# Linear attention, top-1 experts and a dense layer on one core: load order, mask selections, list of output rows and expert 0's preparation rearranged

## The chip, the core and the metric

The kernel runs on one core of a Trainium2 chip. The metric is the device time of one launch in microseconds (us); lower is better. The engines are named as in the profile: PE is TensorE's matmul, PEld its weight load, DVE is VectorE, ACT is ScalarE, POOL is GpSimd, and SP is SyncE, which here only issues transfers (its queue is SPq).

## The reference

Three stages follow each other; the output of each is the input of the next. Sizes: 4 batches, 8 heads, 768 positions, 48 features a head; 3072 tokens of 384 features; 8 experts with 1024 hidden units; a last dense layer with 2048.

```python
for t in range(S):                       # 1. gated linear attention
    state = alpha[:, :, t, :, None] * state + einsum('bhd,bhe->bhde', k[:, :, t], v[:, :, t])
    y[:, :, t] = einsum('bhd,bhde->bhe', q[:, :, t], state)
...
expert_idx = argmax(x @ w_gate, axis=1)  # 2. one expert for each token
gate_w = softmax probability of that expert
out[mask] = gate_w[mask, None] * (maximum(xe @ w1[e], 0.0) @ w2[e])
...
h = x @ w_in                             # 3. dense layer
return (h * sigmoid(h)) @ w_out
```

## The kernel before

**Attention (0 to about 130 us of the span).** The 32 heads are handled as 16 pairs, `p` = 0 to 15, four pairs to a batch. The inputs come in 13 tiles `T` (`place`): four for batch 0, three for each other batch, whose fourth pair is packed into spare partitions of the three and copied out by POOL-queue transfers (`gather_last`, L523). The loop over `p` (from L1014) writes the order of the instructions by hand, and every engine runs its own in that order. For a tile, DVE scans the products of the alphas forwards (`P_SCAN`, L538) and backwards (`R_SCAN`, L556) and scales the keys (`K_SCALE`, L561); POOL scales the queries (`Q_SCALE`, L550). For a pair, PE makes the scores of six chunks of 128 positions in two groups of three (`scores`, L583); they are masked to the lower triangle either by one DVE product (L589) or, for group 0 of pairs 1 to 4 and group 1 of pair 14 (`beside_scans`), by an ACT copy (L602) and a POOL `affine_select` (L606) that is issued after the pair's `Q_SCALE`. PE sums the state updates (`updates`, L619 and L626), DVE scans the states (L636), ACT copies them (L653), and PE makes the outputs (`from_states`, `within`).

**Loads.** All loads go through SP's queue in program order. `load(T, "aqk")` brings the alphas, queries and keys of a tile (12 transfers a tile from tile 4 on), at the top of an iteration; `load_v(p + 3)` brings the values of a pair at the end of iteration `p`. Alphas have 3 buffers, values 4.

**Routing.** When a batch's outputs are there, its logits are made (L712), each token gets its expert and a slot, 512 slots to an expert, from a running count `carry` and the offsets `e512` (`ranks` to `slots2`, L784 to L803). The small sum `cb` (L788) adds the two. A table of the token in each slot (`tab`) is made by one-hot matrices on DVE and six matmuls for each batch (`table`, L834 to L872). The tokens' rows are turned, scaled by their gate and stored to DRAM (`rows`, L915 to L920).

**Hand-over (about 130 to 168 us).** Expert 0 works on its first 192 tokens (`F1(t, 0, CA)` and `S1(t, 0, CA)` for six of its eight weight tiles) while batch 3 is still routed; beside that run the ranking of the experts by size (`turns`), the table in that order (`in_turn`), the splits of the weight tiles into a high and a low part (`w_split`: ACT L331, DVE L332), and three gathers of expert 0's other rows (L346). Those rows are turned by PE and split (`x_tile`: PE L356, ACT L358, DVE L359): tile 1 just before the last `S1`, tiles 2 and 3 after it. Then the columns from 192 on follow.

**Experts and dense layer (to the end).** `F1` (L1211: 9 matmuls into `hp`) and `S1` (L1243: 9 matmuls into three banks) alternate for 64 weight tiles `g`; then `F2` and `S2` for 64 steps of the dense layer. The raw weights stream through four buffers (`next_load`, L327 and L1175 on SP's queue). From step 2 on, one step of the list `late` is issued in each `g` that is not the last of its expert: `offsets`, and then for each of the four batches six steps (`packed`) that make `sidx`, the token of each packed output row, by one-hot matrices on DVE and six matmuls into `pt` (L860). `sidx` is first needed by the scatter of the output (L1444).

The lines at the heart of the change are these.

```python
load_v(p + 3)
...
later = [mask_aside(p, 0)] if beside_scans(p, 0) else []
...
3: [last["in_turn"], lambda: w_split(6), lambda: w_split(7)],
...
late = [offsets] + [f for b in range(B) for f in packed(b)]
```

Of the kernel before, what the change touches and what calls it, by code (L numbers as in the profile page):

```python
# [229 lines left out]
def gla_moe_kernel(  # L230
# [23 lines left out]
    x_f = dr.tile([NP, NC, CH, 2 * D], F32, name="x_f")  # L254

# [112 lines left out]
    gidx = const.tile([128, 4 * E], U32, name="gidx")  # L368
    gidx_a = const.tile([128, 2], U32, name="gidx_a")
# [15 lines left out]
    with actx:  # L385
# [70 lines left out]
        load(2, "k")  # L456
        load_v(2)
        Z1 = ac.tile([128, SP], F32, name="Z1")
# [18 lines left out]
        def constants():  # L477
            nc.gpsimd.iota(iota_i, pattern=[[1, 128]], base=0, channel_multiplier=0)
            nc.gpsimd.iota(prow_i, pattern=[[128, NTILE]], base=0, channel_multiplier=1)
            nc.gpsimd.memset(ones, 1.0)  # L480
            nc.gpsimd.memset(onesf, 1.0)
            nc.gpsimd.memset(tri, -1.0)
            nc.gpsimd.affine_select(
                out=tri, in_=tri, pattern=[[-1, 128]], compare_op=ALU.is_ge, fill=0.0, base=0, channel_multiplier=1
            )
            nc.gpsimd.memset(rmask, 1.0)
            nc.gpsimd.memset(ones8, 1.0)
            nc.gpsimd.memset(rmask[:, :, 0:1], 0.0)
            nc.gpsimd.memset(carry, 0.0)
            nc.gpsimd.tensor_copy(iota_f, iota_i)  # L490
            nc.gpsimd.tensor_scalar(w8, iota_f[:, 0:E], -1.0, float(E), op0=ALU.mult, op1=ALU.add)
            nc.gpsimd.tensor_scalar(e512, iota_f[:, 0:E], float(TM), None, op0=ALU.mult)

        def more_constants():
# [4 lines left out]
            nc.gpsimd.tensor_copy(keys, w8)  # L499
# [100 lines left out]
        def mask_aside(p, g, hs=slice(0, 2)):  # L600
            m = st[p]["m", g][:, hs]
            nc.scalar.copy(m, st[p]["Ap"][:, hs])  # L602
            return lambda: select(m)
# [116 lines left out]
        def route(b):  # L720
# [58 lines left out]
            def ranks():  # L779
# [7 lines left out]
                r["cb"] = rt.tile([128, E], F32, tag="cb", name="cb")  # L787
                nc.vector.tensor_tensor(r["cb"], carry, e512, op=ALU.add)  # L788

            def slots1():  # L790
# [4 lines left out]
                    r["cb"].unsqueeze(2).to_broadcast([128, E, TB]),  # L795
# [32 lines left out]
        def table(bk, sl, b, nhi, acc, res, eng):  # L828
# [35 lines left out]
            def add():  # L864
                if b == 0:
                    nc.vector.tensor_copy(acc, r["pt"])
                elif b < B - 1:
                    nc.vector.tensor_tensor(acc, acc, r["pt"], op=ALU.add)
                else:
                    nc.vector.tensor_tensor(acc, acc, r["pt"], op=ALU.add)  # L870
                    n = 4 if acc is tab else NTILE
                    nc.vector.tensor_scalar(res[:, 0:n], acc[:, 0:n], float(NT - 1), None, op0=ALU.min)  # L872
# [25 lines left out]
        def in_turn():  # L898
# [9 lines left out]
            t = rt.tile([128, E * 4], F32, tag="tt", name="tt", bufs=1)  # L908
            nc.vector.tensor_reduce(t, m.rearrange("p r k e -> p (r k) e"), axis=AX.X, op=ALU.add)
            nc.vector.tensor_scalar(gidx[:, 4:], t[:, 4:], float(NT - 1), None, op0=ALU.min)  # L910
# [103 lines left out]
        for p in range(NP + 1):  # L1014
            on, oy = p < NP, p >= 1
            if p in loads:
                load(loads[p])
# [10 lines left out]
            if on:  # L1028
                ks_transpose(p, 0, 3)
                later = [mask_aside(p, 0)] if beside_scans(p, 0) else []  # L1030
# [24 lines left out]
            if on:  # L1055
                for c in range(3, 6):
                    scores(p, c)
                if beside_scans(p, 1):
                    later.append(mask_aside(p, 1))
# [32 lines left out]
            load_v(p + 3)  # L1092
# [10 lines left out]
    with mctx:  # L1103
# [162 lines left out]
        for step in choose:  # L1266
# [6 lines left out]
            3: [last["in_turn"], lambda: w_split(6), lambda: w_split(7)],  # L1273
# [3 lines left out]
        for t in range(part):  # L1277
# [5 lines left out]
            for step in beside.get(t, []):  # L1283
                step()
            if t == part - 1:
                x_tile(0, 1, CA - 128)
# [5 lines left out]
        x_tile(0, 2, bk=4)  # L1292
        x_tile(0, 3, bk=3)
        for t in range(4, NF):
            next_load()
        F1(*seq[0])
# [7 lines left out]
        off = const.tile([128, E], F32, name="off")  # L1304
# [3 lines left out]
        def offsets():  # L1308
            m = rt.tile([128, E, E], F32, tag="m8", name="m8", bufs=1)
            by_turn(carry, m, cnt)  # L1310
# [4 lines left out]
            nc.vector.tensor_tensor(  # L1315
                m, turn.rearrange("p r e -> p e r"), o.unsqueeze(1).to_broadcast([128, E, E]), op=ALU.mult
            )
            nc.vector.tensor_reduce(off, m, axis=AX.X, op=ALU.add)
# [32 lines left out]
        tabc = const.tile([128, NTILE], F32, name="tabc")  # L1351

        def packed(b):
            r = {}

            def slot():
                co = rt.tile([128, E], F32, tag="cb", name="co")
                nc.vector.tensor_tensor(co, off, e512, op=ALU.subtract)
                t1 = rt.tile([128, E, TB], F32, tag="t1", name="t1")
                nc.vector.tensor_tensor(t1, OH[b], co.unsqueeze(2).to_broadcast([128, E, TB]), op=ALU.mult)  # L1360
                r["s"] = sc = rt.tile([128, TB], F32, tag="sc", name="sc")
                nc.vector.tensor_reduce(sc, t1.rearrange("p e i -> p i e"), axis=AX.X, op=ALU.add)
                nc.vector.tensor_tensor(sc, sc, SLOT[b], op=ALU.add)

            digits, hots, invert, add = table(lambda: 3, lambda: r["s"], b, NTILE, tabc, sidx, nc.vector)
            return [slot, digits, hots, lambda: None, invert, add]

        late = [offsets] + [f for b in range(B) for f in packed(b)]
# [85 lines left out]
        for i, (g, c0, c1) in enumerate(seq):  # L1454
            e, f = divmod(g, NF)
            F1(*seq[i + 1]) if i + 1 < len(seq) else F2(0)
            doubles(g, 1)
# [110 lines left out]
```

## Time and profile before

| what | value |
|---|---|
| time, median of 3 runs | 784.77 us (783.9 to 785.85) |
| the profiled execution, whole | 786.41 us |
| its span, first to last instruction | 784.7 us |
| PE busy | 767.6 us, 98% of the span, 5068 matmuls |
| PEld busy | 698.6 us, 89% |
| DVE busy | 476.9 us, 61% |
| ACT busy | 361.8 us, 46% |
| POOL busy | 160.5 us, 20% |
| mean granted TensorE clock | 0.996 |
| chain that ended last | PE 85%, DMA 5%, DVE 4%, issue 3% |

Busy times are sums over the whole span. The chain is followed back from the last instruction, at each step to what released it. A matmul's end is modelled, so a busy PE is not a PE at its peak; what a step costs is read from the starts of successive groups.

### The profile page before, as it was taken

How to read it: one execution, taken by the hardware profiler on the slowest of the kernel's cores; microseconds unless marked ns; L12 is line 12 of the kernel's file. 1: busy time of each engine (PE TensorE's matmuls, PEld its weight loads, DVE VectorE, ACT ScalarE, POOL GpSimd, SP SyncE). 2: the span in 40 equal slices, each digit the busy share in tenths (PEclk: the TensorE clock that was granted, in tenths of full speed). 3: DMA queues.
4: the chain of work that ended last, by engine and by line, in shares of the span. 5: the costliest groups of instructions: out<-in, count | busy, mean ns of one | idle time of the engine just before them, and what ended most of it. 6: DMA issues, size and time to landing. Idle time of an engine off the chain costs nothing.

```text
span 784.7 us, 13301 instructions
## 1 busy us (share of the span) xinstructions
PE 767.6 (98%) x5068; PEld 698.6 (89%) x5068; DVE 476.9 (61%) x818; ACT 361.8 (46%) x684; POOL 160.5 (20%) x201
## 2 busy tenths in 40 slices
PE   8999899999999999999999999999999999999996
PEld 6887788899999999999899899889899898899896
DVE  8989886657797787788687333343443343343332
ACT  1656466435455545555544334453544445233222
POOL 5754322312242232212112200020020001002002
PEclk9999999999999999999999999999999999999999
DMA  9888893624465555655121110031022001001001
GB/s 231 215 200 215 220 262 112 223 61 138 152 185 169 173 172 171 192 168 184 61 60 33 41 39 18 0 94 36 1 76 53 19 1 40 2 1 41 1 0 45
DMA packets 41642, 80.54 MB, mean 103 GB/s; under 512 B 5640, under 2 KB 19863, under 8 KB 41568
## 3 DMA queue, kind: packets, MB, share of 16 engines
q1 hardware_dynamic: 37568, 67.56, 29.8%
q0 software_dynamic: 4000, 12.03, 5.1%
q8 instruction: 42, 0.69, 0.4%
q14 instruction: 32, 0.26, 0.1%
HBM read 68.03 MB, written 9.44 MB: 99 GB/s over the span
## 4 chain that ended last, share of the span: by engine, by line
PE 85%; DMA 5%; DVE 4%; issue 3%; ACT 1%; SPq 1%; POOL 1%; POOLq 0%; ACTq 0%; DVEq 0%
PE hp L1211 38%; PE both L1422 12%; PE ob L1422 12%; PE both L1243 9%; PE yb L1243 5%; PE Ap L583 2%; PE Yp L664 1%; DVE Pf L538 1%; PE xt L356 1%; PE Yp L679 1%; DMA a__371<-in_alpha_dram 1%; PE Xt L915 1%; DMA E<-in_k_dram 1%; DMA a__1156<-in_alpha_dram 1%; PE Lp L712 1%
## 5 line engine op out<-in xcount | busy, mean ns | idle before, releaser
L1211 PE MATMUL hp<-xh,wh 128*128 128x512 f32 (+10 forms) x498 | 184.0, 371 | 0.4 <-ACT xh L358 0.4
L1211 PE MATMUL hp<-xh,wl 128*128 128x512 f32 (+10 forms) x498 | 184.1, 372 | 0.1
L1400 DVE TENSOR_TENSOR sg<-hp,sg 128x512 f32<-128x512 f32 (+1 forms) x97 | 66.5, 686 | 157.3 <-ACT sg L1399 152.5
L1211 PE MATMUL hp<-xl,wh 128*128 128x512 f32 (+10 forms) x498 | 130.8, 371 | 0.0
L1399 ACT ACTIVATE sg<-hp 128x512 f32<-128x512 f32 (+1 forms) x97 | 57.6, 593 | 154.3 <-PE hp L1211 153.5
L1211 PEld LDWEIGHTS hp<-xl,wh 128*128 128x128 f32 x498 | 91.8, 190 | 13.5
L1211 PEld LDWEIGHTS hp<-xh,wh 128*128 128x128 f32 x498 | 94.1, 189 | 10.5 <-ACT xh L358 0.6
L1211 PEld LDWEIGHTS hp<-xh,wl 128*128 128x128 f32 x498 | 94.4, 190 | 9.5 <-DVE wl L332 0.3
L1410 DVE TENSOR_TENSOR hl<-sg,hh 128x512 fp32r<-128x512 f32 x94 | 65.1, 692 | 61.5 <-PE ob L1422 38.4
L1409 ACT CAST hh<-sg 128x512 fp32r<-128x512 f32 x94 | 58.3, 620 | 70.7 <-DVE sg L1400 70.7
L1223 ACT ACTIVATE hh<-hp 128x464 fp32r<-128x464 f32 (+9 forms) x70 | 34.2, 488 | 114.8 <-PE hp L1211 110.6
L1444 POOL DMA_INDIRECT out_dram<-o,sidx x24 | 24.6, 1023 | 278.9 <-ACT o L1442 274.4
L1138 POOL TENSOR_TENSOR wl<-dx,wh 128x384 fp32r<-128x384 f32 x32 | 39.2, 1225 | 197.7 <-ACT wh L1135 194.2
L332 DVE TENSOR_TENSOR wl<-raw,wh 128x768 fp32r<-128x768 f32 x63 | 62.2, 991 | 7.9 <-ACT wh L331 6.9
L1422 PE MATMUL both<-wh,hh 128*128 128x384 f32 x188 | 64.1, 341 | 0.1
L1422 PE MATMUL both<-wh,hl 128*128 128x384 f32 x188 | 64.0, 340 | 0.0
L1422 PE MATMUL both<-wl,hh 128*128 128x384 f32 x188 | 63.5, 338 | 0.0
L1225 DVE SCALAR_TENSOR_TENSOR hl<-hp,hh 128x464 fp32r<-128x464 f32 (+9 forms) x70 | 38.6, 551 | 40.2 <-ACT hh L1223 39.8
L1422 PE MATMUL ob<-wh,hh 128*128 128x384 f32 x188 | 62.8, 334 | 0.0
L1422 PE MATMUL ob<-wl,hh 128*128 128x384 f32 x188 | 62.8, 334 | 0.0
L1422 PE MATMUL ob<-wh,hl 128*128 128x384 f32 x188 | 62.8, 334 | 0.0
L331 ACT CAST wh<-raw 128x768 fp32r<-128x768 f32 x64 | 52.7, 828 | 0.0
(366 smaller groups left out, 1472.9 us busy)
## 6 DMA issues: line engine op xcount, KB each, us to landing
raw<-in_wt_dram SPq DMA_DIRECT2D x64, 384.0 KB, 3.3
raw<-in_w_dram SPq DMA_DIRECT2D x32, 384.0 KB, 3.1
raw<-in_alpha_dram SPq DMA_DIRECT2D x16, 336.0 KB, 4.1
x_d<-xr SPq DMA_DIRECT2D x24, 192.0 KB, 2.1
E<-in_q_dram SPq DMA_DIRECT2D x18, 144.0 KB, 3.3
E<-in_k_dram SPq DMA_DIRECT2D x18, 144.0 KB, 3.2
E<-E POOLq DMA_DIRECT2D x18, 114.0 KB
E<-in_q_dram SPq DMA_DIRECT2D x4, 336.0 KB, 9.7
```

The costliest lines, as they stand in the source:

```text
L331: nc.scalar.copy(hi, raw[t])
L332: eng.tensor_tensor(lo, raw.pop(t), hi.bitcast(F32), op=ALU.subtract)
L1138: nc.gpsimd.tensor_tensor(r["lo"], r["x"], r["hi"].bitcast(F32), op=ALU.subtract)
L1211: nc.tensor.matmul(hp, lhsT=a[:, kc * 128 : (kc + 1) * 128], rhs=x[:, kc, c0:c1], start=(i == 0), stop=(i == 8))
L1223: nc.scalar.activation(hh[:, :n], hp, AF.Relu)
L1225: nc.vector.scalar_tensor_tensor(hl[:, :n], in0=hp, scalar=0.0, in1=hh[:, :n].bitcast(F32), op0=ALU.max, op1=ALU.subtract)
L1243: nc.tensor.matmul(yb[dc][:, c0:c1], lhsT=a[:, c : c + 128], rhs=b_[:, : c1 - c0], start=(f == 0 and c0 == 0 and i == 0), stop=(f == NF - ...
L1399: nc.scalar.activation(sg[:, z], hp[:, z], AF.Sigmoid)
L1400: nc.vector.tensor_tensor(sg[:, z], hp[:, z], sg[:, z], op=ALU.mult)
L1409: nc.scalar.copy(hh[:, z], sg[:, z])
L1410: nc.vector.tensor_tensor(hl[:, z], sg[:, z], hh[:, z].bitcast(F32), op=ALU.subtract)
L1422: nc.tensor.matmul(yb[tt], lhsT=a[:, tt * 128 : (tt + 1) * 128], rhs=b_[:, 384:768], start=(f == 0 and i == 0), stop=(f == NF2 - 1 and i = ...
```

## The change

- **Load order.** Tile 3's alphas and queries are issued before the values of pair 2, its keys after them. In the loop, a tile's loads move from the top of iteration `p + 1` to the end of iteration `p`; the values go between the alphas and the queries, and they are those of pair `p + 2` instead of `p + 3`.
- **Selections.** The POOL selection of a pair's group becomes two, one for each head. The first is issued before the `Q_SCALE` of the iteration, the second where the whole one stood.
- **Slot counts.** `carry` starts at the experts' offsets instead of 0, so `cb` and its DVE sum go (four times). `e512` is made later on POOL, in `more_constants`, as one more instruction there; `keys` corrects for the offsets.
- **Hand-over.** `x_tile(0, 1)` is issued one step earlier, before the fifth `S1`; `x_tile(0, 2)` before the last `S1`; `x_tile(0, 3)` after it. The splits of weight tiles 6 and 7, with the two loads that follow them, move into the first two steps of the main loop.
- **Output rows.** The four `packed` groups go. Instead, the table in turn order (`ttab`) is turned by one PE transpose, each expert's list of 512 slots is written to DRAM at its packed offset (eight transfers on SP's queue, each with a register read, each list overwriting the unused end of the one before it), the packed list is read back, and one more PE transpose gives `sidx`. These are 43 steps of `late` (three idle ones after each transfer) instead of 25.

```diff
@@ constants and more_constants
-            nc.gpsimd.memset(carry, 0.0)
...
-            nc.gpsimd.tensor_scalar(e512, iota_f[:, 0:E], float(TM), None, op0=ALU.mult)
+            nc.gpsimd.tensor_scalar(carry, iota_f[:, 0:E], float(TM), None, op0=ALU.mult)
...
-            nc.gpsimd.tensor_copy(keys, w8)
+            nc.gpsimd.tensor_scalar(e512, iota_f[:, 0:E], float(TM), None, op0=ALU.mult)
+            nc.gpsimd.tensor_scalar(keys, iota_f[:, 0:E], -1.0 - 8.0 * TM, float(E), op0=ALU.mult, op1=ALU.add)
@@ first loads
         load(2, "k")
+        load(3, "aq")
         load_v(2)
+        load(3, "k")
@@ mask_aside
-            return lambda: select(m)
+            return [lambda h=h: select(m[:, h : h + 1]) for h in range(2)]
@@ ranks, slots1
-                r["cb"] = rt.tile([128, E], F32, tag="cb", name="cb")
-                nc.vector.tensor_tensor(r["cb"], carry, e512, op=ALU.add)
...
-                    r["cb"].unsqueeze(2).to_broadcast([128, E, TB]),
+                    carry.unsqueeze(2).to_broadcast([128, E, TB]),
@@ loop over the pairs
-            if p in loads:
-                load(loads[p])
...
-                later = [mask_aside(p, 0)] if beside_scans(p, 0) else []
+                later = []
+                if beside_scans(p, 0):
+                    sooner, *later = mask_aside(p, 0)
+                    sooner()
...
-            load_v(p + 3)
+            if p + 1 in loads:
+                load(loads[p + 1], "a")
+            if p:
+                load_v(p + 2)
+            if p + 1 in loads:
+                load(loads[p + 1], "qk")
@@ expert 0
-            3: [last["in_turn"], lambda: w_split(6), lambda: w_split(7)],
+            3: [last["in_turn"]],
...
+            if t == part - 2:
+                x_tile(0, 1, CA - 128)
             if t == part - 1:
-                x_tile(0, 1, CA - 128)
+                x_tile(0, 2, bk=4)
             S1(t, 0, CA, [row[2], ranks_and, row[4]] if t == 0 else [])
...
-        x_tile(0, 2, bk=4)
         x_tile(0, 3, bk=3)
-        for t in range(4, NF):
+        for t in range(4, 6):
             next_load()
+        soon = [6, 7]
@@ lists of output rows
+        def clear_slots():
+            t = rt.tile([128, TB, 128], F32R, tag="ol", name="lists", bufs=1).bitcast(F32)
+            lists.update(to=t[0 : 4 * E, 0, :], back=t[0:NTILE, 1, :])
+            nc.gpsimd.memset(t[0:NTILE, 2, :], 0.0)
+            nc.sync.dma_start(slot_d[0:NT].rearrange("(i p) o -> i (p o)", p=128), t[0:NTILE, 2, :])
+
+        def turn_lists():
+            t = bank(3, [4 * E, 128], "tr")
+            nc.tensor.transpose(t, ttab, ident)
+            nc.vector.tensor_copy(lists["to"], t)
+
+        def put_list(e):
+            r = nc.values_load(regs[0:1, e : e + 1], engines=(ET.SP,), min_val=0, max_val=NT)
+            nc.sync.dma_start(
+                slot_d[ds(r, TM)].rearrange("(k p) o -> k (p o)", p=128), lists["to"][4 * e : 4 * e + 4, :]
+            )
+
+        def get_slots():
+            nc.sync.dma_start(lists["back"], slot_d[0:NT].rearrange("(i p) o -> i (p o)", p=128))
+
+        def turn_slots():
+            t = bank(3, [128, NTILE], "tb")
+            nc.tensor.transpose(t, lists["back"], ident[:NTILE, :NTILE])
+            nc.vector.tensor_scalar(sidx, t, float(NT - 1), None, op0=ALU.min)
+
-        late = [offsets] + [f for b in range(B) for f in packed(b)]
+        late = [clear_slots, offsets, turn_lists]
+        for step in [lambda e=e: put_list(e) for e in range(E)] + [get_slots, turn_slots]:
+            late += [step] + [lambda: None] * 3
@@ main loop
             F1(*seq[i + 1]) if i + 1 < len(seq) else F2(0)
+            if soon:
+                w_split(soon.pop(0))
+                next_load()
```

## Rows read from the trace of the kernel before

**Rows 1.** Windows: stretch, its length, each engine's busy us, clock, DMA share, GB/s
```profile
80.00:100.00 20.00, 17.12 (x246) 15.05 (x242) 18.77 (x32) 10.70 (x22) 6.45 (x6) 1.00 0.80 216
180.00:200.00 20.00, 20.00 (x104) 17.68 (x104) 16.01 (x36) 9.89 (x19) 5.68 (x5) 1.00 0.54 166
```
**Rows 2.** Chain of waits, expert steps: start us, us, what, instructions
```profile
174.60 1.89 PE hp L1211 x9
...
178.31 1.88 PE hp L1211 x9
180.20 0.57 PE pt L860 x6
...
182.75 1.90 PE hp L1211 x9
```
**Rows 3.** Timeline of PE at the hand-over: start, us, engine, line, operation, [idle before]
```profile
149.59 0.49 PE L356 MATMUL xt<-ident,xg 128*128 128x128 f32 x3
...
151.07 0.36 PE L1243 MATMUL both<-hl,wh 128*128 128x192 f32 x1 [0.78 <-DVE hl L1225]
...
153.22 0.39 PE L1211 MATMUL hp<-xh,wh 128*128 128x256 f32 x1 [0.44 <-ACT xh L358]
```
**Rows 4.** Timeline of DVE at the hand-over
```profile
148.93 1.82 DVE L332 TENSOR_TENSOR wl<-raw,wh 128x768 fp32r<-128x768 f32 x2
150.67 0.35 DVE L1225 SCALAR_TENSOR_TENSOR hl<-hp,hh 128x192 fp32r<-128x192 f32 x1
```
**Rows 5.** Timeline of POOL at the hand-over, the last of expert 0's three gathers
```profile
147.36 0.98 POOL L346 DMA_INDIRECT xg<-x_d,gidx  x1 [0.30 <-issue]
```
**Rows 6.** Timeline of PEld at the hand-over, row tile 3 of expert 0
```profile
152.38 0.26 PEld L356 LDWEIGHTS xt<-ident,xg 64*128 64x128 f32 x3 [0.19 <-DMA xg<-x_d,gidx]
```
**Rows 7.** Windows of 1 us behind the hand-over
```profile
154.00:155.00 1.00, 1.00 (x7) 1.00 (x7) 0.00 (x0) 0.00 (x0) 0.88 (x1) 0.50 1.02 406
```
**Rows 8.** Chain of waits behind the hand-over
```profile
153.22 3.90 PE hp L1211 x18
...
158.21 1.08 PE hp L1211 x9
```
**Rows 9.** Timeline of DVE in attention, pair 10
```profile
84.64 1.77 DVE L538 TENSOR_TENSOR_SCAN Pf<-a__1156,Z 128x774 f32<-128x774 f32 x1 [0.85 <-DMA E<-in_k_dram]
...
86.56 1.60 DVE L788 TENSOR_TENSOR cb<-carry,e 128x8 f32<-128x8 f32 x1
...
88.18 0.94 DVE L589 TENSOR_TENSOR Am<-Ap,mask 128x768 f32<-128x768 f32 x1
```
**Rows 10.** Timeline of POOL in attention, pair 10
```profile
86.50 1.63 POOL L550 TENSOR_TENSOR E<-E,Pf 128x768 f32<-128x768 f32 x1 [8.03 <-DVE Pf L538]
```
**Rows 11.** Timeline of PE in attention, pairs 10 and 11
```profile
85.13 0.94 PE L583 MATMUL Ap<-E 48*128 48x128 f32 x12
...
89.18 1.01 PE L583 MATMUL Ap<-E 48*128 48x128 f32 x12 [1.20 <-DVE Am L589]
```
**Rows 12.** Timeline of SP's queue in attention, alphas of tile 11
```profile
86.30 1.79 SPq L439 DMA_DIRECT2D a__1289<-in_alpha_dram  x4
```
**Rows 13.** The alphas of tile 11: from issue to landing
```profile
DMA to landing us min/median/max: 4.1/4.3/4.4
```
**Rows 14.** The state updates, those of pair 11: ns, first and last start
```profile
L619 PE MATMUL U<-v__1154,kst x10: 208/208/243, 94.4 to 94.9; 128*48 128x48 f32 x10
```
**Rows 15.** Timeline of DVE in attention, key scalings of tiles 3 and 6
```profile
27.59 1.45 DVE L561 TENSOR_TENSOR E<-E,Rv 112x768 f32<-112x768 f32 x1
...
47.98 0.94 DVE L561 TENSOR_TENSOR E<-E,Rv 128x768 f32<-128x768 f32 x1
```
**Rows 16.** Timeline of POOL in attention: a constant, then pair 1's selection
```profile
22.45 1.51 POOL L499 COPY keys<-w 128x8 f32<-128x8 f32 x1
...
25.89 2.34 POOL L606 TENSOR_SCALAR_AFFINE_SELECT Am<-Am 128x768 f32<-128x768 f32 x1
```
**Rows 17.** Waits of SP's queue: us in total, times, longest
```profile
SPq L327 <- DVE wl L332: 50.8, 21, 3.9
```

More of the change, by code (lines that the diff above doesn't have):

```diff
@@ L254, in gla_moe_kernel @@
     x_f = dr.tile([NP, NC, CH, 2 * D], F32, name="x_f")
+    slot_d = dr.tile([NT + TM, 1], F32, name="slot_d")
     def two_banks(name):
@@ L368, in gla_moe_kernel @@
     gidx = const.tile([128, 4 * E], U32, name="gidx")
+    ttab = const.tile([128, 4 * E], F32, name="ttab")
     gidx_a = const.tile([128, 2], U32, name="gidx_a")
@@ L598, in beside_scans, with mask_aside @@
             return (p, g) == (NP - 2, 1) or g == 0 and 1 <= p <= 4
-        def mask_aside(p, g, hs=slice(0, 2)):
-            m = st[p]["m", g][:, hs]
-            nc.scalar.copy(m, st[p]["Ap"][:, hs])
-            return lambda: select(m)
+        def mask_aside(p, g):
+            m = st[p]["m", g]
+            nc.scalar.copy(m, st[p]["Ap"])
+            return [lambda h=h: select(m[:, h : h + 1]) for h in range(2)]
         def select(m):
@@ L870, in add @@
                     nc.vector.tensor_tensor(acc, acc, r["pt"], op=ALU.add)
-                    n = 4 if acc is tab else NTILE
-                    nc.vector.tensor_scalar(res[:, 0:n], acc[:, 0:n], float(NT - 1), None, op0=ALU.min)
+                    nc.vector.tensor_scalar(res[:, 0:4], acc[:, 0:4], float(NT - 1), None, op0=ALU.min)
             return [digits, hots, invert, add]
@@ L907, in in_turn @@
             )
-            t = rt.tile([128, E * 4], F32, tag="tt", name="tt", bufs=1)
-            nc.vector.tensor_reduce(t, m.rearrange("p r k e -> p (r k) e"), axis=AX.X, op=ALU.add)
-            nc.vector.tensor_scalar(gidx[:, 4:], t[:, 4:], float(NT - 1), None, op0=ALU.min)
+            nc.vector.tensor_reduce(ttab, m.rearrange("p r k e -> p (r k) e"), axis=AX.X, op=ALU.add)
+            nc.vector.tensor_scalar(gidx[:, 4:], ttab[:, 4:], float(NT - 1), None, op0=ALU.min)
         def rows(b, c):
@@ L1058, in gla_moe_kernel @@
                 if beside_scans(p, 1):
-                    later.append(mask_aside(p, 1))
+                    later += mask_aside(p, 1)
                 for step in later:
@@ L1301, in gla_moe_kernel @@
         gather(1)
-        off = const.tile([128, E], F32, name="off")
         inc8 = const.tile([128, E], F32, name="inc8")
@@ L1309, in offsets @@
             m = rt.tile([128, E, E], F32, tag="m8", name="m8", bufs=1)
-            by_turn(carry, m, cnt)
+            nc.vector.tensor_tensor(inc8, carry, e512, op=ALU.subtract)
+            by_turn(inc8, m, cnt)
             nc.vector.tensor_tensor_scan(inc8, ones8, cnt, 0.0, op0=ALU.mult, op1=ALU.add)
@@ L1314, in offsets @@
             nc.vector.tensor_copy(regs[:, 0:E], o)
[L1315 to L1318, printed above, removed]
         def read_offset(e):
@@ L1350, in gla_moe_kernel @@
         sidx = const.tile([128, NTILE], U32, name="sidx")
[L1351 to L1366, printed above, removed]
-        late = [offsets] + [f for b in range(B) for f in packed(b)]
+        lists = {}
+        def clear_slots():
[21 more added lines that the diff above has]
+            late += [step] + [lambda: None] * 3
         def y_store(e):
```

## The prediction

> **What bounds the kernel now.** I read the windows first, then the chain of waits, then the timelines where the chain leaves PE. From about 170 us to the end PE never pauses; the window 180 to 200 us is one of many alike, with PE busy for all 20 us and DVE for 16.01 [rows 1]. There only fewer or shorter matmuls save time. In attention the chain changes between PE and DVE; in the window 80 to 100 us DVE is busy for 18.77 of 20 us and PE for 17.12, so a DVE delay costs its length until PE is next in line [rows 1]. Between the two lies the hand-over, where PE waits for DVE, ACT and a gather. So the change is priced in three places. I make the sum against the profiled span, 784.7 us; the whole execution took 786.41, and the median of the runs, 784.77, happens to lie beside the span, so I subtract the same saving from the median.
>
> **The change part by part.**
>
> *Output rows.* A step of the experts without extras runs from 174.60 to 178.31, 3.71 us; the next, which holds one of the four groups of six `pt` matmuls, runs to 182.75, 4.44 us [rows 2]. A group thus costs 0.73 us, four cost 2.9; by the group's own 0.57 they would cost 2.3. Two PE transposes come in. One of the six matmuls takes 0.57 / 6, about 0.1 us, so I charge 0.2 for two, 0.4 at most. Net: 2.7 gained, between 1.9 and 2.9. The one-hot work on DVE also goes; DVE had 4 of 20 us free there, so I count nothing for it. The clearing write, the eight lists and the read add ten transfers to SP's queue. A list waits for the one before it to land, and the raw weight loads queue behind it; a late weight reaches PE through the splits on ACT and DVE. A transfer of 3 KB to DRAM has no row; the nearest is an alpha load with 4.3 us to landing [rows 13]. Three idle steps of 3.7 us lie between two lists, so that wait should be over before it is met. The same holds for the last transpose, which waits for the read to land with all of PE queued behind it: four steps, some 14 us, against 4.3. SP also has room: its weight loads themselves waited 50.8 us for a buffer to be emptied, the longest wait 3.9 [rows 17]. I take 0 for the ten; from below nothing can be gained, from above each could cost PE its landing less that room, 4.3 - 3.9 = 0.4, so 4 us.
>
> *Hand-over.* DVE ran two splits of 1.82 us together from 148.93, and the product `hl` that PE needed came only behind them at 150.67 [rows 4]; PE waited 0.78 us for it, until 151.07 [rows 3]. The splits (weight tiles 6 and 7) move to where DVE has room, so this wait goes. Next in line is the gather: PE's load for row tile 3 waited 0.19 us for it, until 152.38 [rows 6], 5.0 us after its issue at 147.36 [rows 5]. Now the transposes of tile 1 are asked for before the fifth `S1`, which is nine matmuls or about 1.0 us ahead of 149.59 [rows 3], and tile 2's before the last one. Two weight loads fewer compete with the gathers, but if tile 1's rows land only at 149.5, PE waits up to 0.9 us there and the gain is given back. Two of the three row tiles are then split beside `S1`; for the last one PE still waits for ACT, as before (0.44) [rows 3]. I take 0.78 + 0.19, less 0.1 for the gathers: 0.9 gained, between 0 and 1.3. The moved splits and their loads are hidden by PE's matmuls of the first two main steps; without that cover they would cost their 1.82.
>
> *Clock.* Just behind these waits the granted clock was 0.50, the lower level of 1.2 GHz [rows 7]. The 18 matmuls there took 3.90 us, against 1.08 for nine of the same shape at the full clock [rows 8]: 3.90 - 2.16 = 1.7 us lost. Before the fall PE had idled for 0.78 and 0.44 us [rows 3]. With the first wait gone I expect the clock to stay, and count 1.7; the other end is 0.
>
> *Slot sum and the wait in iteration 10.* The sum `cb` is 8 columns, yet took 1.60 us at 86.56 [rows 9], because POOL's query scaling held from 86.50 to 88.13 [rows 10]. It goes, and what follows it on DVE is a copy out of PSUM and the masking product, which also reads PSUM (0.94 us [rows 9]); if POOL held these up as well, only the wait ahead of them would be gained. For there the forward scan waited 0.85 us for alphas [rows 9]. These now go ahead of the values, with one load of 288 KB less before them: at 216 GB/s [rows 1] that is 1.3 us earlier, so the wait goes too. Together DVE could be 2.4 earlier at 88.18, but PE's scores end only at 85.13 + 0.94 = 86.07 [rows 11], so the product cannot come before 86.1: 2.1 gained, of which PE takes 1.2 at once (its wait for that product [rows 11]) and the rest behind the state scan. I take 2.0. What is late next is a load: the alphas of tile 11 are issued from 86.30 to 88.1 [rows 12] and land 4.3 later [rows 13], and the values of pair 11 now come right behind them, so they land at about 92.4; PE wants them at 94.4 [rows 14] less 2.0. That just meets. The other end, with every such load 1.5 late, is 0.5 gained.
>
> *Selections.* In pairs 1 to 3 a key scaling, 0.94 us when free (47.98), took 1.45 [rows 15] because the POOL selection, 25.89 to 28.23, was still running [rows 16]: 0.5 each, 1.5 in all. Half a selection behind `Q_SCALE` would end before it. But the other half comes ahead of `Q_SCALE`, and meets the forward scan there; POOL small instructions beside that scan took 1.51 us instead of a fraction [rows 16]. `Q_SCALE` then ends later and holds up the backward scan. In pair 1, POOL also has the additional constant ahead of it. By the rows the selection's time is moved from one DVE instruction to another: I take 0.2 lost, between 1.5 gained and 1.0 lost. Pair 14's selection is only cut in two, with nothing ahead of it; I count 0.
>
> The Trainium skill, "SBUF — State Buffer", section "Who interferes with whom", has a rule for it: a VectorE instruction with two SBUF inputs contends with a GpSimd instruction that reads SBUF, and whichever starts first holds the shared ports for its whole length. The rows of the key scaling (0.51 us longer) agree. By that rule halves shorten no hold in sum, which speaks against this edit; if holds did not matter for the first half, the sum would be 1.7 better.
>
> *Loads otherwise.* Values come an iteration later, and no longer wait for a buffer of the pair before; SP is not blocked. I count 0.
>
> Sum: 2.7 + 0.9 + 1.7 + 2.0 - 0.2 = 7.1 us. 784.7 - 7.1 = 777.6 for the span, and 784.77 - 7.1 = **777.7** for the median.
>
> **The rivals.**
>
> *The hand-over does not pay.* The gathers land late, PE idles there and the clock falls all the same: 0.9 and 1.7 are lost, 780.3 us. For it speaks that one gather took 5.0 us; against it, that two of the four loads beside them go.
>
> *The loads become the bound in attention.* With DVE faster, values and alphas arrive when PE and DVE already wait: only 0.5 of the 2.0 stays, 779.2 us. DMA was busy for 0.80 of the window [rows 1], which is near enough.
>
> *The halves free the key scalings.* Three key scalings are 0.5 shorter and nothing else is longer: 1.5 gained instead of 0.2 lost, 776.0 us. Against it: the 1.51 us of a small POOL instruction beside the scan [rows 16].
>
> *The steps were not PE's.* If DVE or ACT set the length of an expert step, taking matmuls away would shorten nothing, and that part does not do what it says: 780.4 us. PE's 20.00 of 20 us [rows 1] speaks against it.
>
> *Slower: the lists hold up the weights.* SP's queue is in order, and each of the ten transfers may make the following weight loads late by its landing, 4.3 us [rows 13], if SP's room is not there when it is needed. From 0.71 us of PE waiting for each on, the 7.1 us are used up; at 1.2 us each the time is 789.7. Against it: no wait of PE for a split or a raw load is seen in these steps.
>
> **How the numbers follow.** The forecast has 0.5, the hand-over 0.18, the loads 0.15, the halves 0.07, the steps 0.05, the slower case 0.05. The likeliest time is 777.7. Downwards the best ends (2.9, 1.3, 1.7, 2.1, and 1.5 by the selections) give 9.5, so 775.3. Upwards, the hand-over and the loads together cost 4.1 of the 7.1: 781.8. Beyond lie the slower case and mixtures with it or with the steps case, less than 2 in 10. A difference of 0.3%, 2.4 us, is about what a measurement of this kernel can tell from none; faster than 782.4 are all cases but the slower, 0.95, less 0.09 for mixtures that pass it: 0.86; within 0.3% 0.09, slower 0.05.
>
> **What would show it.** In the profile after: no `pt` group behind 170 us and steps there of 3.7 us throughout; no wait of PE for `hl` and a full clock around 153 us; no `cb`, and no DVE wait for alphas near 84 us; key scalings of pairs 1 to 3 near 1.0 us, but backward or forward scans beside them longer than 1.76. The prediction is wrong if the main loop starts no earlier against the end of attention, if PE shows waits for `v`, or if weight splits wait for raw loads beside the lists.

## The result, and the profile after

The changed kernel took **777.98 us** (median of 4 runs, 777.49 to 778.2), against 785.31 for the kernel before (4 runs): ratio 0.9909, 95% interval 0.9882 to 0.9936. Run again later, in e9 below, it took 780.62 us (12 runs) against 784.80: ratio 0.9955, interval 0.9931 to 0.9978. So the change gains 7 us in the first measurement and 4 in the second; by the intervals that is 5.0 to 9.3 and 1.7 to 5.4 us, which just overlap. The forecast of 777.7 agrees with the first, and the experiments below show that its terms agree less well than its sum.

The profiled execution of the changed kernel has a span of 776.5 us (778.2 whole). The surest way to see where 8.2 us of span went is to note when the same work starts in both traces:

| landmark | before, us | after, us | gained so far |
|---|---|---|---|
| first `F1` of expert 0 | 134.37 | 131.87 | 2.50 |
| first `F1` of the main loop | 153.22 | 150.46 | 2.76 |
| first `S1` of the main loop | 156.91 | 152.71 | 4.20 |
| first `F1` with 448 columns | 167.89 | 163.70 | 4.19 |
| last matmul | 777.79 | 770.82 | 6.97 |

The last 1.2 us of the span's gain lie behind the last matmul, where the last rows are stored and the program ends. So: attention 2.50, hand-over 0.26, the two `F1` behind it 1.44, experts 2.78, the end 1.2.

Two of these need a remark. Of attention's 2.50, 0.14 only says that the first query load landed earlier in this execution (DVE's first scaling starts at 6.44, before at 6.58). And the end, from the last matmul's end to the end of the span, takes 6.2 to 6.6 us in the three profiles with `pt` groups (before, e1, e6), and 5.3 to 5.8 in the eleven without. So some of it seems to go with the output rows; no experiment looks at why.

**Hand-over.** Timeline of PE after (start, us, engine, line, operation, [idle before, releaser]); the answers to [rows 3, 6]:

```profile
147.40 0.49 PE L357 MATMUL xt<-ident,xg 128*128 128x128 f32 x3
...
149.65 0.40 PE L357 MATMUL xt<-ident,xg 64*128 64x64 f32 x3 [0.44 <-DMA xg<-x_d,gidx]
150.46 0.39 PE L1217 MATMUL hp<-xh,wh 128*128 128x256 f32 x1 [0.41 <-issue]
...
163.70 0.37 PE L1217 MATMUL hp<-xh,wh 128*128 128x448 f32 x1
...
770.64 0.33 PE L1438 MATMUL ob<-wl,xh 128*128 128x384 f32 x1
770.82 0.34 PE L1438 MATMUL ob<-wh,xl 128*128 128x384 f32 x1
```

The wait for `hl` is gone. In its place PE waits longer for the last of the three gathers, and then, as before, for ACT's cast (the row names no releaser, but the cast ended at 150.40). Timeline of POOL after, that gather's issue, the answer to [rows 5]:

```profile
144.87 0.97 POOL L347 DMA_INDIRECT xg<-x_d,gidx  x1 [0.30 <-issue]
```

Counted from the first `F1`, it is issued at 13.00 us (before: 147.36 - 134.37 = 12.99), and its rows land 4.8 us later (before 5.0). Windows after: stretch, its length, busy us of PE, PEld, DVE, ACT, POOL, clock, DMA share, GB/s; the answer to [rows 7]:

```profile
152.00:153.00 1.00, 1.00 (x11) 1.00 (x10) 0.42 (x1) 0.31 (x2) 0.10 (x1) 1.00 0.43 146
154.00:155.00 1.00, 1.00 (x11) 1.00 (x10) 0.96 (x1) 0.01 (x1) 0.00 (x0) 1.00 0.00 0
```

The granted clock is 1.00 here, where it had been 0.50.

**Attention.** Timeline of DVE after, pair 1's scan and key scaling, then the alpha scan and the masking product of iteration 10, the answers to [rows 15, 9]:

```profile
25.48 2.72 DVE L560 TENSOR_TENSOR_SCAN Rv<-a__158,D 112x774 f32<-112x774 f32 x1
28.23 1.09 DVE L565 TENSOR_TENSOR E<-E,Rv 112x768 f32<-112x768 f32 x1
...
34.58 1.09 DVE L565 TENSOR_TENSOR E<-E,Rv 128x768 f32<-128x768 f32 x1
...
83.01 1.76 DVE L542 TENSOR_TENSOR_SCAN Pf<-a__1156,Z 128x774 f32<-128x774 f32 x1
...
84.91 0.15 DVE L868 COPY tab<-pt 128x32 f32<-128x32 f32 x1
85.42 0.96 DVE L593 TENSOR_TENSOR Am<-Ap,mask 128x768 f32<-128x768 f32 x1 [0.36 <-PE Ap L587]
```

The alpha scan no longer waits for a load, `cb` is gone, and the masking product comes at 85.42, 2.76 us earlier than before. It now waits for the scores, as forecast. The copy and the product, which read PSUM, are not held up by POOL's query scaling, which ran from 84.86 to 86.49. Timeline of ACT after, where it waits for stores of turned rows (`x_d`):

```profile
70.78 0.58 ACT L918 ACTIVATE xr<-Xt,gt 128x384 f32<-128x384 f32 x1 [0.69 <-DMA x_d<-xr]
...
116.28 0.58 ACT L918 ACTIVATE xr<-Xt,gt 128x384 f32<-128x384 f32 x1 [3.00 <-DMA x_d<-xr]
```

Before, the first of these waits was 2.54 us and the second was for PE. The first row's shorter wait gave PE 0.62 us, between 72 and 79 us; the second row's longer one took back 0.5, between 118 and 126. The prediction named neither.

**Experts.** Timeline of ACT after; these are two expert steps, the second of which held a `pt` group before:

```profile
176.04 0.56 ACT L1229 ACTIVATE hh<-hp 128x464 fp32r<-128x464 f32 x1 [1.35 <-PE hp L1217]
...
179.80 0.56 ACT L1229 ACTIVATE hh<-hp 128x464 fp32r<-128x464 f32 x1 [2.04 <-PE hp L1217]
```

The step is 3.76 us long; it was 4.45. The four steps lose 0.69, 0.64, 0.67 and 0.67, together 2.68.

### The profile page after: what moved, and what is told of

The parts are those of the page before. It is cut to its first block, busy times and chain, and to the rows that moved or that the text cites. A ratio compares the mean times of both kernels' runs of the same rounds, so it can differ in the third digit from the quotient of the medians.

```text
span 776.5 us, 13258 instructions
## 1 busy us (share of the span) xinstructions
PE 761.3 (98%) x5046; PEld 693.2 (89%) x5046; DVE 463.1 (60%) x766; ACT 361.5 (47%) x684; POOL 165.4 (21%) x207
```

## The experiments

Times are medians; a ratio is to the kernel before on the same chip (784.93 us for e1 to e4, 785.95 for e5 to e8, 784.80 for e9 to e12). The other columns are read from the timelines of PE and the windows of each profile.

| run | time, us | ratio, 95% interval | first `F1` | from it to the main loop | first 448-column `F1` to last matmul | clock near 0.5 before the last matmul, at |
|---|---|---|---|---|---|---|
| before | 784.77 | | 134.37 | 18.85 | 609.90 | 153 to 157 |
| after | 777.98 | 0.9909, 0.9882 to 0.9936 | 131.87 | 18.59 | 607.12 | nowhere |
| e1 | 781.56 | 0.9956, 0.9937 to 0.9975 | 131.57 | 18.52 | 609.93 | 13 to 16 |
| e2 | 778.20 | 0.9916, 0.9893 to 0.9940 | 130.72 | 18.84 | 607.50 | nowhere |
| e3 | 782.01 | 0.9965, 0.9951 to 0.9980 | 134.77 | 18.44 | 607.52 | 68 to 72 |
| e4 | 778.64 | 0.9926, 0.9897 to 0.9955 | 132.42 | 18.74 | 607.15 | nowhere |
| e5 | 782.69 | 0.9955, 0.9936 to 0.9975 | 132.54 | 19.61 | 607.53 | 14 to 18 |
| e6 | 786.86 | 1.0011, 0.9991 to 1.0032 | 137.33 | 19.57 | 609.81 | 118 to 125 |
| e7 | 781.21 | 0.9940, 0.9922 to 0.9958 | 131.43 | 19.54 | 607.50 | 152 to 155 |
| e8 | 780.55 | 0.9931, 0.9907 to 0.9956 | 131.31 | 19.59 | 607.53 | 151 to 157 |
| e9 | 780.62 | 0.9955, 0.9931 to 0.9978 | 133.93 | 19.58 | 607.53 | 153 to 157 |
| e10 | 780.79 | 0.9945, 0.9923 to 0.9968 | 132.22 | 19.52 | 607.28 | nowhere |
| e11 | 781.94 | 0.9959, 0.9939 to 0.9979 | 133.02 | 19.53 | 607.26 | 153 to 157 |
| e12 | 778.38 | 0.9923, 0.9895 to 0.9950 | 130.82 | 17.73 | 607.26 | nowhere |

**e1: output rows undone.**

```diff
...
-        late = [clear_slots, offsets, turn_lists]
...
+        late = [offsets] + [f for b in range(B) for f in packed(b)]
```

> The changed kernel with one part undone: the tokens of the output rows come again from one-hot matrices and four groups of six pt matmuls; no lists go to DRAM. Theory (an expert step is as long as PE's work): four steps are 0.64 to 0.69 us longer, 2.7 in sum, and the two transposes go, which the trace shows with 0.08 and 0.30; so 2.3 us longer than the changed kernel, 780.3. Prediction's sum: 2.7 longer, 780.7. Rival (the steps are not PE's): 778.0, no step longer.

The expert stage alone is the sharpest measure: 609.9 us in the three profiles with `pt` groups (before, e1, e6), 607.1 to 607.5 in the eleven without, so 2.3 to 2.8 us. Timeline of PE in e1, first 448-column `F1` and last matmul:

```profile
163.27 0.37 PE L1218 MATMUL hp<-xh,wh 128*128 128x448 f32 x1
...
773.20 0.34 PE L1432 MATMUL ob<-wh,xl 128*128 128x384 f32 x1
```

The median, 3.6 above the changed kernel's, agrees within the intervals; in the profiles, 0.9 us more lie behind the last matmul (6.25 against 5.34). The rival falls.

**e2: hand-over undone.**

```diff
-            3: [last["in_turn"]],
+            3: [last["in_turn"], lambda: w_split(6), lambda: w_split(7)],
...
-            if t == part - 2:
-                x_tile(0, 1, CA - 128)
             if t == part - 1:
-                x_tile(0, 2, bk=4)
+                x_tile(0, 1, CA - 128)
...
```

> The changed kernel with the hand-over as before: splits 6 and 7 ahead of the hidden product, row tiles 1 and 2 turned later. Theory from the two traces (the last gather, issued 13.0 us behind the first F1 in both, sets the start of the main loop): the main loop starts 0.26 us later against the first F1, 18.85 instead of 18.59, and the clock falls to 0.50 behind it, which costs 1.5: 1.75 us longer, 779.7. Prediction's sum: 0.9 and 1.7, 780.6. Rival (the clock fell for another reason than this idling): 0.26 longer, 778.2, clock 1.00 at 150 to 156 us.

From the first `F1` to the main loop 18.84 us, 0.25 more than after; the ratio is 0.9916 against 0.9909. And with the old wait for `hl` back, at 0.78 us as before, the clock did not fall. Timeline of PE and windows of e2:

```profile
147.41 0.36 PE L1249 MATMUL both<-hl,wh 128*128 128x192 f32 x1 [0.78 <-DVE hl L1231]
...
149.56 0.39 PE L1217 MATMUL hp<-xh,wh 128*128 128x256 f32 x1 [0.47 <-ACT xh L359]
```

```profile
151.00:152.00 1.00, 1.00 (x11) 1.00 (x10) 0.42 (x1) 0.33 (x1) 0.21 (x1) 1.00 0.93 375
```

**e3: load order undone.**

```diff
...
+            if p in loads:
+                load(loads[p])
...
-            if p + 1 in loads:
-                load(loads[p + 1], "a")
-            if p:
-                load_v(p + 2)
-            if p + 1 in loads:
-                load(loads[p + 1], "qk")
+            load_v(p + 3)
```

> The changed kernel with the loads in the old order: a whole tile's alphas, queries and keys at the top of an iteration, values of pair p + 3 at its end. Theory from the traces: ACT waits again about 2.5 us for a store of turned rows near 70 us, which delays PE by 0.62; the forward scan near 83 us waits again 0.85 for alphas; on the other side the late stores near 113 to 117 us, which cost 0.45, come earlier: about 1.0 us longer, 779.0. Prediction's sum: only the wait for alphas, and what the missing slot sum leaves of it, 0.5 to 0.9 longer. Rival (the order of loads is hidden anyway): 778.0.

4.0 us longer than the changed kernel's first measurement, and 3.8 longer than e2, which ran beside it on the same chip: far more than the prediction gave to the loads. Timelines of DVE, of ACT and of SP's queue in e3:

```profile
63.33 1.77 DVE L540 TENSOR_TENSOR_SCAN Pf<-a__853,Z 128x774 f32<-128x774 f32 x1 [0.72 <-DMA a__853<-in_alpha_dram]
```

```profile
73.40 0.58 ACT L916 ACTIVATE xr<-Xt,gt 128x384 f32<-128x384 f32 x1 [2.54 <-DMA x_d<-xr]
...
104.07 0.58 ACT L916 ACTIVATE xr<-Xt,gt 128x384 f32<-128x384 f32 x1 [3.62 <-DMA x_d<-xr]
```

```profile
98.22 1.80 SPq L441 DMA_DIRECT2D E<-in_k_dram  x4
100.12 0.84 SPq L918 DMA_DIRECT2D x_d<-xr  x2
```

An alpha wait is there, at another place than before; but the long waits are ACT's, for stores. Before the second wait, the store of the rows that ACT had scaled at 91.45 is issued only at 100.12, behind the key loads on the queue. A fall of the clock at 68 to 72 us, beside the first wait, adds to this execution.

**e4: the slot sum back.**

```diff
...
+                nc.vector.tensor_tensor(r["cb"], carry, carry, op=ALU.max)
...
```

> The changed kernel with an 8-column sum back in the place of cb, as the maximum of carry with itself (the value is carry). Theory: near 85 us it starts while POOL scales the queries, takes about 1.6 us, and delays the masking product by 1.2 (which now waits 0.36 for the scores); in iteration 14 it costs 0.25 more: 1.4 us longer, 779.4, of which up to 0.45 may be swallowed at 120 us. Prediction's sum: 1.4 as well (2.0 less the part of the loads). Rival (the sum took 1.60 us only because it came late, not because of POOL): 0.13 us long, 778.2.

Timeline of DVE in e4:

```profile
84.79 1.61 DVE L787 TENSOR_TENSOR cb<-carry 128x8 f32<-128x8 f32 x1
```

So 8 columns take 1.61 us again beside the query scaling, and the masking product comes 1.00 later than after. Counted from the same start, that is 1.1 us, and the fourth sum in iteration 14 adds 0.2. By 125 us most of the lead of after is gone (0.25 us is left), since after lost time to a store at 116 and this execution did not. The median, 0.7 above, can't be told from either case; the cost is shown by the trace alone.

**e5: values early again, alphas still first.**

```diff
-            if p:
-                load_v(p + 2)
+            load_v(p + 3)
```

> The changed kernel, but the values of pair p + 3 are again loaded at the end of iteration p; the alphas stay ahead of them. It parts the two halves of the new load order, which cost 4.0 us together when undone. Theory A (the 288 KB that come one pair later are what counts, because the stores of turned rows and the queries and keys stand behind them on SP's queue, and ACT waits for those stores): most of the 4.0 comes back, 780 to 782 us, and ACT waits 2.5 us or more for a store near 70 us. Theory B (alphas ahead of values are what counts, as in the prediction): 778 to 778.5 us, and neither DVE nor PE waits more than in the changed kernel.

Inconclusive: its time is 1.5 and 2.1 us above e7 and e8 on the same chip, as theory A has it, but its profile shows no wait of DVE for a load, and only 1.04 us of ACT for a store, as theory B has it. The profiled execution was the fastest of its ten.

**e6: the hand-over alone, in the kernel before.** The edit is the reverse of e2's.

> The kernel before with the new hand-over alone (splits 6 and 7 in the first two main steps, row tiles 1 and 2 turned earlier). Prediction's sum: 2.6 us faster than the kernel before, and the clock at 150 to 158 us is 1.00. Theory after undoing it (the last gather sets the start of the main loop, and the falls of the clock come at places that change from execution to execution): 0.2 to 0.3 us faster, not to be told from the kernel before, 18.6 us instead of 18.85 from the first F1 to the main loop.

The ratio, 0.9991 to 1.0032, leaves out a gain of 2.6 us (0.9967). The clock fell in this execution too, elsewhere. Windows of e6:

```profile
120.00:122.00 2.00, 2.00 (x29) 1.69 (x28) 0.41 (x1) 0.80 (x1) 0.45 (x1) 0.50 0.31 107
```

**e7: selections whole.**

```diff
-            return [lambda h=h: select(m[:, h : h + 1]) for h in range(2)]
+            return [lambda: select(m)]
...
-                    sooner, *later = mask_aside(p, 0)
-                    sooner()
+                    later = mask_aside(p, 0)
```

> The changed kernel with each selection whole again and behind the query scaling. Prediction's sum: 0.2 us faster than the changed kernel; the traces say 0.06, so no difference can be measured: 778.0. In the trace the key scalings of pairs 1 to 3 take 1.43 to 1.45 us again instead of 1.09, and the scan ahead of them 1.94 and 1.75 instead of 2.72 and 1.9. Rival (the halves free the key scalings, 1.5 us): 779.5.

Timeline of DVE in e7, tile 4:

```profile
32.32 1.75 DVE L560 TENSOR_TENSOR_SCAN Rv<-a__371,D 128x774 f32<-128x774 f32 x1
34.10 1.44 DVE L565 TENSOR_TENSOR E<-E,Rv 128x768 f32<-128x768 f32 x1
```

Scan and scaling together take 3.19 us whole and, after, 1.90 + 1.09 = 2.99 in halves; in pair 1 it is 3.39 before and 2.72 + 1.09 = 3.81 after. Twice 0.2 gained, 0.4 lost: nothing. First `F1` at 131.43 lies among the others. The rival's 1.5 us are not seen there. The median, 3.2 above, decides nothing: the changed kernel was not run on this chip, the hand-over is 1.0 longer in all four profiles from it, and the profile of e7 holds a fall of the clock.

**e8: all lists in one step.**

```diff
...
-        for step in [lambda e=e: put_list(e) for e in range(E)] + [get_slots, turn_slots]:
-            late += [step] + [lambda: None] * 3
+        late = [clear_slots, offsets, turn_lists, all_lists] + [idle] * 35 + [turn_slots]
```

> The changed kernel with the eight lists and the read issued in one step, without idle steps between them; the last transpose stays where it was. So SP meets every landing at once. Slower rival of the prediction (each transfer holds up the weights by its landing, about 4.3 us): SP stands still for 9 x 4.3 = 39 us, four raw buffers cover some 15 us, and PE waits 20 us or more: 798 or worse. Prediction's case (the landing is short, and SP's queue has room): the raw loads come up to some 10 to 20 us late, PE waits 0 to 5 us: 778 to 783. The rows of SP show what one list takes until the next can go.

Timeline of SP's queue in e8:

```profile
172.59 9.78 SPq L1370 DMA_DIRECT2D slot_d<-lists  x8
183.30 0.33 SPq L1375 DMA_DIRECT2D lists<-slot_d  x1
183.83 0.40 SPq L328 DMA_DIRECT2D raw<-in_wt_dram  x1
```

A list goes every (9.78 - 0.33) / 7 = 1.35 us, not 4.3, and in this time SP mostly reads the list's register and issues: it waited for the landing of a list for 0.2 us in all, and the read waited 0.9 for the last one. The next raw load is issued only at 183.83, and PE still waits for nothing: the expert stage takes 607.53 us, as in e5 and e9. The slower rival falls even without the idle steps.

**e9 to e12: the changed kernel on a third chip, six buffers for turned rows, and raw loads held back.** e9 has no edit. e10, e11 (with e3's edit) and e12 have the first line; e12 also has the rest.

```diff
-            xr = xp.tile([128, 4, 2, D], F32, tag="xr", name="xr", bufs=4)
+            xr = xp.tile([128, 4, 2, D], F32, tag="xr", name="xr", bufs=6)
...
-        for t in range(4, 6):
-            next_load()
         soon = [6, 7]
...
-        late = [clear_slots, offsets, turn_lists]
+        clear_slots()
+        for t in range(4, 6):
+            next_load()
+        late = [lambda: None, offsets, turn_lists]
```

> The changed kernel itself, as the measure for the three other runs of this call, which share its chip. 777.5 to 781 us; 6 to 7.5 us faster than the kernel before on the same chip. If falls of the clock come by chance of the execution, its executions do not all have the same mean clock.

Timeline of ACT, timeline of PE and windows of e9:

```profile
103.07 0.58 ACT L918 ACTIVATE xr<-Xt,gt 128x384 f32<-128x384 f32 x1 [4.47 <-DMA x_d<-xr]
```

```profile
151.29 0.40 PE L357 MATMUL xt<-ident,xg 64*128 64x64 f32 x3 [0.36 <-DMA xg<-x_d,gidx]
153.51 0.58 PE L1217 MATMUL hp<-xh,wh 128*128 128x256 f32 x1 [1.83 <-ACT xh L359]
```

```profile
154.00:155.00 1.00, 1.00 (x7) 1.00 (x7) 0.00 (x0) 0.00 (x0) 0.29 (x1) 0.50 0.04 15
```

The same kernel as after, with an ACT wait of 4.47 us for a store, a hand-over 1.0 longer, and the fall of the clock that the change was thought to remove. This execution, at 783.09 us one of the slowest of its twelve, shows where the second measurement can lose against the first, not what each of its executions lost. The new order of loads does not keep the stores free either: here, too, they are issued behind alphas, queries and keys (98.80, the keys from 96.90).

> The changed kernel with six instead of four buffers for the turned rows (xr), so that ACT need not wait for the store of the fourth row group before. Theory A (ACT's waits for stores of turned rows are what the order of loads acts on): ACT shows no wait for a store, and the first F1 comes 0.4 to 1.2 us earlier than in the changed kernel on this chip: 0.3 to 1.2 us faster. Theory B (those waits are covered): same time.

No wait of ACT for a store is left, and the time is that of e9. But the executions differ by when the first query load lands: DVE's first scaling starts at 6.50 in e10, at 6.11 in e9. Counted from that start, the first `F1` comes at 127.82 in e9, 125.72 in e10, 124.96 in e12, and 124.80 to 125.43 where ACT's waits were 3.0 us or less (after, e1, e2, e7, e8). So the buffers cover late stores, but a typical execution has little to cover. The median bears out theory B, the profiles A for bad cases only.

> The changed kernel with the loads in the old order, and six buffers for the turned rows. Undoing the load order cost 4.0 us. Theory A (the old order costs its time through ACT, which waits 2.5 and 3.6 us for stores that stand behind loads on SP's queue): at least 2 of the 4.0 come back, so 1 to 2 us longer than the changed kernel on this chip, what is left being the wait of DVE for alphas. Theory B (the old order costs its time by late alphas, values and queries): still 3 to 4 us longer than the changed kernel.

1.3 us longer than e9 and 1.2 longer than e10. That is theory A's range and short of theory B's, though the intervals of the ratios overlap. From the first scaling to the first `F1` it takes 126.69 us against 129.04 in e3, no wait of ACT for a store is left, and what is left is DVE's wait for alphas. Timeline of DVE in e11:

```profile
85.13 1.77 DVE L540 TENSOR_TENSOR_SCAN Pf<-a__1160,Z 128x774 f32<-128x774 f32 x1 [1.80 <-DMA a__1160<-in_alpha_dram]
```

> The changed kernel with six buffers for the turned rows, and with the raw weight loads of the hand-over held back on SP's queue until expert 1's gathers are issued, so that expert 0's last gather has the DMA engines for itself. Theory (the last gather sets the start of the main loop, and lands late because raw loads of 384 KB are issued beside it): the gather lands 0.5 us or more earlier, PE does not wait for it, and the main loop starts 0.4 to 0.9 us earlier against the first F1 than in the changed kernel; 0.4 to 0.9 us faster than six buffers alone. Rival (the held loads come too late for the splits of the first main steps): PE waits there, slower by 1 us or more.

Timelines of POOL (the last gather of expert 0), of PE, of ACT and of SP's queue in e12:

```profile
143.80 0.98 POOL L347 DMA_INDIRECT xg<-x_d,gidx  x1 [0.30 <-issue]
```

```profile
147.75 0.40 PE L357 MATMUL xt<-ident,xg 64*128 64x64 f32 x3
148.55 0.38 PE L1217 MATMUL hp<-xh,wh 128*128 128x256 f32 x1 [0.41 <-ACT xh L359]
```

```profile
148.18 0.32 ACT L359 CAST xh<-xt 128x192 fp32r<-128x192 f32 x1 [0.83 <-PE xt L357]
```

```profile
152.14 3.49 SPq L328 DMA_DIRECT2D raw<-in_wt_dram  x4
```

PE no longer waits for the gather, which landed within 3.95 us of its issue (4.4 to 5.0 in the thirteen other profiles), and the main loop starts 17.73 us behind the first `F1`, 1.8 earlier than in e9 and e10. Of this, 0.4 to 0.6 us come from the gather and 1.2 to 1.4 from ACT's cast, which also starts at once. The edit moves the clearing write ahead as well, so the raw loads are not alone. The median is 2.4 us below e10's on the same chip, more than expected. Of its 7 timed executions one had a mean clock of 0.996 or less, against 9 of 12 in e10. It is the fastest version on its chip.

## Why the prediction was right, and where it was not

| term | forecast | the two traces | experiments |
|---|---|---|---|
| output rows | 2.7 | 2.78 | 2.3 to 2.8 |
| hand-over wait | 0.9 | 0.26 | 0.25 |
| clock | 1.7 | 1.44 | not shown to be the change's |
| slot sum, alpha wait | 2.0 | 1.13 + 0.93 | 1.1 for the sum |
| selections | -0.2 | -0.06 | none |
| loads otherwise | 0 | 0.62 - 0.5 | up to 4 with the order |
| end, behind the last matmul | not named | 1.2 | 0.9 in e1 |

**Output rows: right.** Step length, PE as its owner and SP's room held. The two transposes took 0.08 and 0.30 us (the second with 0.3 of waiting), 0.38 where 0.2 was taken. A list, which is 4 rows of 128 values, 2 KB and not the 3 KB of the prediction, costs SP 1.35 us, not the 4.3 of the nearest row. Of the 2.78, 0.35 lie in six late steps in which the same 370-column matmuls were each some 0.003 us shorter, which no row explains.

**Hand-over: the step that failed is "this wait goes"**, with 0.78 counted as gained. The wait for `hl` went, but the gather of tile 3 was the true bound: in all fourteen profiles it is issued 12.98 to 13.00 us behind the first `F1`, whatever PE does in between, so PE merely spent the same time waiting for it. The prediction weighed tile 1's gather, and from [rows 6] took only 0.19 us for the last one. From landing to main loop it is 153.22 - 152.38 = 0.84 before and 150.46 - 149.65 = 0.81 after. What could be gained was an earlier landing, and e12 gains 0.4 to 0.6 us by one. The rival that fits is the prediction's first, that the hand-over does not pay: its 780.3 us lie beside the second measurement.

**Clock: the step that failed is to read one execution as the kernel's.** The 1.44 us came in the first pair of traces, and the mechanism (PE idles, the clock falls) fits e12. But e2 kept the old waits and the full clock; e7, e8, e9 and e11 have the new hand-over and the fall. Of the fourteen profiles, nine show a fall before the last matmul: five directly behind the hand-over, four elsewhere. Idling seems to count, but does not decide: ahead of the main loop PE idled for 2.1 to 2.2 us in all in e5 to e11, mostly by ACT's late cast, and four of these seven fell there; in the other seven it idled for 0.4 to 1.3, and only the kernel before fell. The timed runs agree that the falls were not removed: on the chip of e9, 12 of 30 executions of the kernel before and 6 of 12 of the changed kernel had a mean clock of 0.996 or less. So no run shows that the 1.7 was the change's to give. With the 0.64 missing at the hand-over it would make up 2.3 of the 2.9 us by which the second measurement falls short of the 7.1; that this is what it lacks is argued, not shown.

**Slot sum and alphas: right**, term by term: the wait gave 0.93, the sum 1.13, and the scores became the limit at 85.42. Not counted was the second `cb` on the path, in iteration 14, worth 0.25 more.

**Loads otherwise: the step that failed.** The prediction followed loads to DVE and PE and found no wait. But the stores of turned rows share SP's queue, and ACT, with four buffers, waits for them; PE then waits for ACT. That made the load order worth up to 4 us (e3), and of the 3.8 us by which e3's attention was longer than the typical one (129.04 against some 125.2 from the first scaling), 2.3 are not there in e11, whose stores have room. Not all of the 2.3 need be the stores': e3 also had its fall of the clock there, and e11 had not. With six buffers, on another chip, the order is worth 1.3 us, and with four the changed kernel itself can meet the long wait (e9). So the size stays open between 1 and 4. The rival of the late loads looked at the right queue and the wrong transfers.

**Selections: right.** The time moved from the scaling into the scans. The Trainium skill, "SBUF — State Buffer", section "Who interferes with whom", says that a VectorE instruction with two SBUF inputs contends with a GpSimd instruction that reads SBUF. The traces agree: half a selection takes 2.0 us beside a scan and 0.52 without, and halves gave no gain. Timeline of POOL after, a half beside the masking product, which reads PSUM, and a half beside a scan:

```profile
24.46 0.52 POOL L610 TENSOR_SCALAR_AFFINE_SELECT Am<-Am 128x384 f32<-128x384 f32 x1
...
32.88 1.98 POOL L610 TENSOR_SCALAR_AFFINE_SELECT Am<-Am 128x384 f32<-128x384 f32 x1
```

So the sum was right in part by luck. Undone one at a time on one chip, the rows, the hand-over, the load order and the slot sum cost 3.6, 0.2, 4.0 and 0.7 us against the changed kernel's first measurement, 8.5 together, where the whole change gave 7.3: a load order worth more than forecast stood against a hand-over and a clock worth less. In the pair of traces it was another coincidence: there the hand-over's missing 0.64 was made up by the 1.2 us at the end, which nobody had forecast, and the clock's 1.44 came from a fall in the one execution profiled before.

## What to carry to other kernels

A wait that goes is worth only the time until the next thing that lands; find the row that sets that landing, and ask what issues it. When loads are reordered, follow every transfer on the queue, stores too, to the engine that waits for its buffer. A fall of the clock, or a late load, seen in one execution is not a property of the kernel until a second profile shows it at the same place.

## What was not expected of the hardware

- **The clock falls at changing places.** e1 and after issue the same instructions until 150 us; e1 fell to 0.50 at 13 to 16 us, after did not. The Trainium skill, "TensorE: Matmul & The Clock Gate", section "What's actually happening", says that the activity window runs freely and does not restart with a kernel; that the same waits have different ends here agrees with it.
- **ACT's cast of the last row tile starts late on two of the chips.** In e10 the transposes start at 149.72 and last 0.40, and the cast starts at 151.36; in e5 to e11 the gap from the end of the transposes is 0.9 to 1.45 us; in after and e1 to e4, with raw loads in flight as well, it is not there, and with the loads held back (e12) it is gone. No row shows what ACT waits for; the cause stays open.
- **The first query load** lets DVE's first scaling start between 5.73 and 7.52 us in fourteen profiles, and shifts all of attention with it.
- **A small instruction beside POOL's query scaling** is held up with one SBUF input too. Timeline of DVE in e10, whose query scaling ran from 86.52 to 88.15; the same instruction takes 0.17 elsewhere:

```profile
87.28 0.90 DVE L810 TENSOR_SCALAR sm<-sm 128x6 f32<-128x6 f32 x1
88.21 0.19 DVE L812 RECIPROCAL gt<-sm 128x6 f32<-128x6 f32 x1
```
